# Rearranging the seams of a fused Fourier-mixing and mixture-of-experts kernel: start-up constants, the last two batches, the first expert tiles

## The chip, the cores and the metric

The kernel runs on one core of one Trainium2 chip. The metric is the device time of one execution in microseconds; lower is better. Beside the time stands a profile of one execution, with every instruction of the engines: PE (matrix multiply) with its weight loads PEld, DVE (VectorE), ACT (ScalarE), POOL (GpSimd), and the DMA queue of SP (SyncE).

## What is computed

Eight sequences of 2496 tokens with 256 channels go through a real Fourier transform along the sequence, a complex linear mix with a soft threshold, and the inverse transform. The 19968 result rows are tokens for a mixture of eight experts; each token goes to one expert, two matrix products with a ReLU between.

```python
X = np.fft.rfft(x, axis=1)
Yr = Xr @ w_r - Xi @ w_i + b_r
Yi = Xr @ w_i + Xi @ w_r + b_i
Yr = np.sign(Yr) * np.maximum(np.abs(Yr) - lam, 0.0)   # Yi likewise
y = np.fft.irfft(Yr + 1j * Yi, n=x.shape[1], axis=1)
...
logits = x @ w_gate + modality_bias[modality_id]
e_idx = np.argmax(logits, axis=1)
for e in range(E):
    h = np.maximum(x[mask] @ w1[e], 0.0)
    out[mask] = gate_w[mask, None] * (h @ w2[e])
```

## The kernel before

**Number format.** Products that need accuracy are made of three: a value is split into a high half (rounded copy, by ACT or DVE) and a low half (the value less its high half), and high·high, high·low and low·high are summed in PSUM.

**The Fourier part** runs over 8 batches (`b`). The transform is factored: `s1_chunk` (first forward stage, 11 chunks a batch, two batches ahead, its result stored to the DRAM scratch `scr` through the staging tile `ev`), `s2_pair` (second forward stage), the mix (`mix_bias`, `mix_shared`, `mix_own`, `shrink`), `is2_group` (first inverse stage, into the SBUF tile `z`), then 22 `pivot`s (transpose with the second inverse stage's split) and 22 `is1` (last stage and gate logits). A batch has a forward phase of five groups `g`, each with two pairs `m` and `m+1`, and then a pivot phase. The order of PE, ACT, DVE and POOL instructions is the order in which the code issues them; SP's order is set by the compiler's own schedule.

**PSUM.** Tags x (second forward stage), y (mix), z (first inverse stage and pivots) and r (last stage, routing) have two banks each. Odd pivots share y with the mix for `j < 16` and in the last two batches (line 369).

**Constants.** At `b == 0`, `g == 1` the generators `rt.consts()` and `at.consts_last()` take two tiles of the ring `ev` (three buffers in pool `w3`) as staging and load them by SP (lines 414, 196); at `g == 3` DVE copies them out and the buffers are free.

**Routing** of batch `b` (`Route.route`) is a generator of 14 small steps, mostly on DVE, run during batch `b+1`: `route()` takes one step unless the last one ended with "pe" (the next has a PE instruction); such a step waits until after `mix(m+1)` (lines 1141 to 1153). When it is done, 22 indirect DMAs a batch (`scatter`, POOL, line 548) write the rows of that batch, sorted by expert, into DRAM `xs`. For batch 5 the generator `tiles_early` (the table of expert tiles) follows the routing in the same chain; what is left of a chain goes on one step a pivot. `fence` makes SP wait for all scatters so far.

**Expert weights** are split by `SplitWeights.step` in 64 pieces: ACT makes the high half, POOL (in the forward groups) or DVE (in the pivot phase) the low half, two stores to DRAM `wsp` follow, and the next raw piece is loaded. Batch 7 has six of the steps.

**Seam between batches 6 and 7.** The banks y are held by odd pivots until the end of the pivot phase, so `mix_bias` for pairs 72 and 73 stands after the last pivot of batch 6; `fill` puts two matmuls of no use before it.

**Expert part** (`Experts.run`): 78 tiles of 256 tokens. SP loads the weights of tile 0, the tokens of tiles 0 to 3, and then, ordered behind the last scatter of batch 6 (line 927), the weights of tile 1. `prep` transposes a tile (DVE), makes its high half `xh` (ACT) and its low half `xl` (POOL, line 800); `ffn` has 48 matmuls from `xh` and `xl` (line 820) and 48 for the second product (line 850). The routing of batch 7 and its scatters run beside the first expert tiles. The pools of the expert part reuse the SBUF addresses of the Fourier part.

Of the kernel before, what the change touches and what calls it, by code (L numbers as in the profile page):

```python
# [128 lines left out]
class Attn:  # L129
# [5 lines left out]
    def pools(self, ctx):  # L135
        tc, nb = self.tc, self.nb
        pool = lambda name, bufs, **k: ctx.enter_context(tc.tile_pool(name=name, bufs=bufs, **k))

        self.w6 = pool("w6", 6)
        self.w3 = pool("w3", 3)  # L140
        self.wx = pool("wx", 3)
        self.ww = pool("ww", 2)
        self.wo = pool("wo", 2)
        self.cp = pool("consts", 1)
        self.w4 = pool("w4", 4)
        self.w2 = pool("w2", 2)
# [146 lines left out]
    def s2_pair(self, b, p, at):  # L293
        nc = self.nc
        ps = self.ps.tile([128, 2, 2, 2, N2], F32, tag="x", name=f"s2_{b}_{p}")
        for i in range(2):
            k1 = 2 * p + i
            for c in range(2):
                nc.tensor.matmul(ps[:, c, :, i, :], at[:, i, c * 128:(c + 1) * 128],
                                 self.m[:, k1 * 128:(k1 + 1) * 128].rearrange("p (r k) -> p r k", r=2),  # L300
                                 start=True, stop=True)
        ps = ps.rearrange("p c r i k -> p c r (i k)")
        us = self.w2.tile([128, 2, 128], F32, tag="Us", name=f"Us_{b}_{p}")
        xh = self.w3.tile([128, 2, 2, 128], F32R, tag="Xh", name=f"Xh_{b}_{p}")
        xl = self.w3.tile([128, 2, 2, 128], F32R, tag="Xl", name=f"Xl_{b}_{p}")
        nc.scalar.copy(us, ps[:, :, 0, :])
        nc.scalar.copy(xh, ps)
        nc.vector.tensor_add(us, us, ps[:, :, 1, :])
        nc.vector.tensor_sub(xl, ps, xh)
        return us, xh, xl  # L310

    def mix_bias(self, b, p):

        ps = self.ps.tile([128, 2, 256], F32, tag="y", name=f"mx_{b}_{p}")
        if b == self.nb - 1 and p in (2, 3):
            self.fill(ps)
        self.nc.scalar.copy(ps[:, 0, :], self.bias[:, 0, :])
        return ps

    def fill(self, ps):  # L320

        w = self.w.rearrange("p i c h d -> p (i c h d)")
        self.nc.tensor.matmul(ps.rearrange("p i d -> p (i d)"), w[:, :128], w[:, :512], start=True, stop=True)

# [23 lines left out]
    def is2_group(self, b, g, ss):  # L348

        nc = self.nc  # L350
        if g == 0:
            self.z = self.w1.tile([128, 2 * N2, K1, 2], F32, tag="z", name=f"z_{b}")
        ps = [self.ps.tile([128, 2, 2, 128], F32, tag="z", name=f"zs_{b}_{g}_{i}") for i in range(2)]
        for h, s in enumerate(ss):
# [11 lines left out]
    def pivot(self, b, j):  # L366
        nc = self.nc
        base = min(3 * j, N2 - 3)
        tag = "y" if j % 2 and (j < 16 or b >= self.nb - 2) else "z"
        ps = self.ps.tile([128, 512], F32, tag=tag, name=f"pv_{b}_{j}")  # L370
# [347 lines left out]
class Experts:  # L718
# [72 lines left out]
    def prep(self, i):  # L791
# [7 lines left out]
        nc.scalar.copy(xh, tr)  # L799
        nc.gpsimd.tensor_sub(xl, tr, xh)  # L800
        ix = self.x.tile([128, 2], I32, tag="ix", name=f"ix_{i}")
# [3 lines left out]
    def ffn(self, i, xh, xl, ix, between):  # L805
# [5 lines left out]
        for p in range(4):  # L811
# [4 lines left out]
            for q in range(2):  # L816
                f = 2 * p + q
                ops = [(lo, c, x) for lo, x in ((0, xh), (0, xl), (1, xh)) for c in range(2)]
# [182 lines left out]
def build(tc, I, out, nb):  # L1001
    nc = tc.nc
    with ExitStack() as outer:
        dp = outer.enter_context(tc.tile_pool(name="wsp", bufs=1, space=DRAM))
        wsp = dp.tile([E * 128, 8192], F32, name="wsp")
        with ExitStack() as ctx:
# [85 lines left out]

            state = None
            routing = iter(())

            def route(n=1):
                nonlocal state
                for _ in range(n):
                    if state != "pe":
                        state = next(routing, None)  # L1100

            for b in range(nb):
                done = b == nb - 1
                for g in range(5):
                    m = 10 * b + 2 * g + 2
                    if g or not b:
                        shared(m)
                        route()
                        shared(m + 1)
                    ins = load(m + 2) or ins  # L1110
                    ins = load(m + 3) or ins
                    if b == 0:
                        with tc.issue_after(ins.ins):
                            if g < 2:
                                at.table_load("m", g + 3)
                            if g < 4:
                                at.table_load("q", g + 1)
                            if g == 1:
                                late = [rt.consts(), at.consts_last()]
                            if g in (1, 3):  # L1120
                                for t in late:
# [19 lines left out]
                    due = state == "pe"  # L1141
# [6 lines left out]
                    if not due:  # L1148
# [3 lines left out]
                    if due:  # L1152
                        state = next(routing, None)
                    if g < 4:
                        bias(m + 2)
# [4 lines left out]
                    s2(m + 3)  # L1160
                    if g < 4:
# [7 lines left out]
                    route()  # L1169
# [11 lines left out]
                for j in range(J):  # L1181
# [9 lines left out]
                    if j == (20 if b + 2 < nb else J - 1):  # L1191
# [7 lines left out]
                for _ in routing:  # L1199
                    pass  # L1200
                shared(10 * b + 12)
                shared(10 * b + 13)
                for jj, r in pend:
# [47 lines left out]
```

## Time and profile before

| what | value |
|---|---|
| median of 3 runs | 1535.38 us (1535.17 to 1539.0) |
| profiled execution | 1536.55 us, of which the span from first to last instruction is 1534.8 us |
| PE busy | 1469.2 us (96%) |
| DVE, ACT, POOL busy | 722.9, 657.8, 510.7 us |
| pivot phases of batches 6 and 7 begin | 533.80 and 595.25 us |
| first expert matmul | 615.32 us |

Rows show a start, a duration, engine, line, operation and tiles; in square brackets the idle time before the instruction and what ended it. A `PEclk` of 1.00 or 0.50 is the granted TensorE clock: 2.4 or 1.2 GHz. A window row has the busy time of every engine in the stretch and, in brackets, how many instructions began there.

### The profile page before, as it was taken

The numbers are of one execution on the slowest core, as the hardware profiler recorded it, in microseconds if no ns is written. First come the engines' busy times: TensorE is split into PE (matmuls) and PEld (weight loads), VectorE is DVE, ScalarE is ACT, GpSimd is POOL, SyncE is SP. The second block draws the span as 40 slices with busy tenths as digits, with TensorE's granted clock in tenths as the row PEclk, the third lists the DMA queues.
The fourth block names the chain that finished last, engine by engine and source line by source line (L and its number), as shares of the span: only waits on it lengthen the run. The fifth ranks groups of instructions, "written<-read, shape, count | busy, mean of one in ns | idle before, by whom it ended". The sixth has DMA issues, their size and how long they took to land. (4 is left out here: it accounts for less than half of the span.)

```text
span 1534.8 us, 35125 instructions
## 1 busy us (share of the span) xinstructions
PE 1469.2 (96%) x12458; PEld 1420.7 (93%) x12458; DVE 722.9 (47%) x1546; ACT 657.8 (43%) x1375; POOL 510.7 (33%) x511
## 2 busy tenths in 40 slices
PE   4789999999999999799999999999999998999998
PEld 2689999999999988699999999999999998999998
DVE  3657767676776665343333333333333333333332
ACT  3347677777667556232323323232323222233232
POOL 0001344444445454335523223222322223223222
PEclk8899999999999999899999999999999999999999
DMA  6847687879786677423434325552225238626440
GB/s 193 250 140 239 223 272 229 285 227 295 229 266 193 199 223 224 160 54 79 129 69 115 90 51 162 156 156 43 57 43 161 49 63 302 207 41 199 122 145 35
DMA packets 289718, 244.58 MB, mean 159 GB/s; under 512 B 208448, under 2 KB 243980, under 8 KB 285289
## 3 DMA queue, kind: packets, MB, share of 16 engines
q1 hardware_dynamic: 270549, 200.73, 45.2%
q0 software_dynamic: 18992, 41.58, 8.1%
q8 instruction: 100, 1.64, 0.5%
q14 instruction: 77, 0.63, 0.1%
HBM read 432.83 MB, written 100.08 MB: 347 GB/s over the span
## 5 line engine op out<-in xcount | busy, mean ns | idle before, releaser
L850 PE MATMUL y<-w,hh 128*128 128x256 f32 x2496 | 433.3, 277 | 2.0 <-DMA w<-wsp 1.5
L820 PE MATMUL h<-xh,w 128*128 128x256 f32 x2496 | 403.7, 278 | 4.5 <-DMA w<-wsp 3.4
L850 PEld LDWEIGHTS y<-w,hh 128*128 128x128 f32 x2496 | 377.3, 188 | 2.8 <-ACT hh L822 2.3
L850 PE MATMUL y<-w,hl 128*128 128x256 f32 x1248 | 346.5, 278 | 0.1
L820 PEld LDWEIGHTS h<-xh,w 128*128 128x128 f32 x2496 | 340.2, 189 | 5.0 <-issue 3.6
L823 DVE SCALAR_TENSOR_TENSOR hl<-h,hh 128x512 fp32r<-128x512 f32 x312 | 209.5, 690 | 239.3 <-ACT hh L822 238.0
L863 POOL DMA_INDIRECT out<-o,ix x161 | 158.7, 985 | 429.8 <-ACT o L842 392.5
L820 PE MATMUL h<-xl,w 128*128 128x256 f32 x1248 | 245.7, 278 | 10.3 <-POOL xl L800 10.3
L822 ACT ACTIVATE hh<-h 128x512 fp32r<-128x512 f32 x312 | 178.7, 597 | 162.9 <-PE h L820 162.9
L850 PEld LDWEIGHTS y<-w,hl 128*128 128x128 f32 x1248 | 234.2, 188 | 0.8 <-DVE hl L823 0.3
L820 PEld LDWEIGHTS h<-xl,w 128*128 128x128 f32 x1248 | 189.8, 189 | 10.5 <-POOL xl L800 10.5
L840 DVE TENSOR_SCALAR o<-y,xt 128x256 f32<-128x256 f32 x78 | 37.8, 484 | 317.1 <-ACT o L842 313.0
L842 ACT ACTIVATE o<-y,xt 128x256 f32<-128x256 f32 x78 | 37.2, 477 | 345.7 <-PE y L850 345.7
L800 POOL TENSOR_TENSOR xl<-tr,xh 128x512 fp32r<-128x512 f32 x78 | 101.0, 1294 | 187.5 <-ACT xh L799 187.4
L548 POOL DMA_INDIRECT xs<-x1b,si x88 | 87.8, 998 | 83.8 <-ACT ph L378 30.5
L548 POOL DMA_INDIRECT xs<-x,si x88 | 87.8, 998 | 69.1 <-ACT u L344 25.4
L373 PE MATMUL pv<-pv,z 128*120 128x136 f32 x704 | 109.0, 279 | 1.8 <-DVE mid L455 1.8
L337 PE MATMUL mx<-wmix,Xh 128*128 128x256 f32 x640 | 104.8, 285 | 1.6 <-DVE mx L330 1.6
L373 PEld LDWEIGHTS pv<-pv,z 128*120 128x120 f32 x704 | 97.4, 182 | 8.2 <-ACT z L364 2.1
L379 DVE TENSOR_TENSOR pl<-pv,ph 120x264 fp32r<-120x264 f32 x176 | 76.0, 432 | 55.6 <-ACT ph L378 51.3
L995 POOL TENSOR_TENSOR wl<-wr,wh 128x512 fp32r<-128x512 f32 x46 | 59.1, 1286 | 124.7 <-ACT wh L994 118.9
L799 ACT CAST xh<-tr 128x512 fp32r<-128x512 f32 x78 | 48.5, 622 | 107.6 <-DVE ix L802 93.6
(191 smaller groups left out, 2119.9 us busy)
## 6 DMA issues: line engine op xcount, KB each, us to landing
w<-wsp SPq DMA_DIRECT2D x166, 2048.0 KB
a<-scr SPq DMA_DIRECT2D x80, 256.0 KB
xt<-xs SPq DMA_DIRECT2D x624, 32.0 KB
wr<-in_moe_w SPq DMA_DIRECT2D x64, 256.0 KB
wsp<-wh SPq DMA_DIRECT2D x64, 256.0 KB
wsp<-wl SPq DMA_DIRECT2D x64, 256.0 KB
scr<-ev SPq DMA_DIRECT2D x98, 160.0 KB
x<-in_x SPq DMA_DIRECT2D x96, 156.0 KB
```

The source lines that it names most:

```text
L337: self.nc.tensor.matmul(ps[:, i, :], t[:, c, 1 - i, :], self.w[:, i, c, lo, :], start=False, stop=n == len(ops) - 1, skip_group_check=True)
L373: nc.tensor.matmul(ps[:PK, c * 128:c * 128 + D // 2 + E], self.z[:, o:o + 3, :, :].rearrange("p n k r -> p (n k r)"), self.pv[:, c, :], st ...
L379: nc.vector.tensor_sub(pl, ps[:PK, :GC], ph)
L548: i = self.nc.gpsimd.indirect_dma_start(out=self.xs, out_offset=bass.IndirectOffsetOnAxis(ap=si[:, k:k + 1], axis=0), in_=rows, in_offset= ...
L799: nc.scalar.copy(xh, tr)
L800: nc.gpsimd.tensor_sub(xl, tr, xh)
L820: nc.tensor.matmul(ps[:, q, :], w1[:, lo, c, f * 128:(f + 1) * 128], x[:, c, :], start=n == 0, stop=n == 5)
L822: nc.scalar.activation(hh[:, 2 * p:2 * p + 2, :], ps, AF.Relu)
L823: nc.vector.scalar_tensor_tensor(hl[:, 2 * p:2 * p + 2, :], ps, 0.0, hh[:, 2 * p:2 * p + 2, :], ALU.max, ALU.subtract)
L850: nc.tensor.matmul(y[s], lhsT, w2[:, lo, f, :], start=n == 0, stop=n == 23)
L863: ins = self.nc.gpsimd.indirect_dma_start(out=self.out, out_offset=bass.IndirectOffsetOnAxis(ap=ix, axis=0), in_=o, in_offset=None, bounds ...
L995: eng.tensor_sub(lo, raw, hi)
```

## The change

- `xl` of expert tiles 0 and 1 is made by DVE, and tile 0 adds its low-half products last.
- The constants' generators start at `g == 2` and end at `g == 4`.
- In batches 6 and 7 (the last two) odd pivots use the banks x; batch 7's last group of `is2_group` uses x too. The pairs 72 and 73 get their bias in group 4 of batch 6, and `shared` for them stands before batch 6's pivots. `fill` is gone.
- Routing: a "pe" step is released by a count of `stage()` calls, six in a group, when it is over 2; in the last two batches three of the places in a group take two steps (`fast`).
- Weight splits: none in batch 7; batch 5 has seven instead of six in its groups; the pivot phases of batches 1 to 5 have three instead of two.
- Tiles `Xh` and `Xl` move to a pool of their own, `wX`, at other SBUF addresses.

```diff
+        self.wX = pool("wX", 3)
...
-        xh = self.w3.tile([128, 2, 2, 128], F32R, tag="Xh", name=f"Xh_{b}_{p}")
+        xh = self.wX.tile([128, 2, 2, 128], F32R, tag="Xh", name=f"Xh_{b}_{p}")
...
-        if b == self.nb - 1 and p in (2, 3):
-            self.fill(ps)
...
+        tag = "x" if b == self.nb - 1 and g == 4 else "z"
+        ps = [self.ps.tile([128, 2, 2, 128], F32, tag=tag, name=f"zs_{b}_{g}_{i}") for i in range(2)]
...
-        tag = "y" if j % 2 and (j < 16 or b >= self.nb - 2) else "z"
+        last = b >= self.nb - 2
+        tag = ("x" if last else "y") if j % 2 and (j < 16 or last) else "z"
...
-        nc.gpsimd.tensor_sub(xl, tr, xh)
+        (nc.gpsimd if i > 1 else nc.vector).tensor_sub(xl, tr, xh)
...
+                terms = ((0, xh), (0, xl), (1, xh)) if i else ((0, xh), (1, xh), (0, xl))
+                ops = [(lo, c, x) for lo, x in terms for c in range(2)]
...
+            def stage(n=1):
+                nonlocal state, age
+                age += n
+                if state == "pe" and age > 2:
+                    state, age = next(routing, None), 0
...
+                    fast = 1 + (b >= nb - 2)
                     if g or not b:
                         shared(m)
                         route()
+                        stage()
                         shared(m + 1)
+                        stage()
...
-                            if g == 1:
+                            if g == 2:
                                 late = [rt.consts(), at.consts_last()]
-                            if g in (1, 3):
+                            if g in (2, 4):
...
-                    route()
+                    route(fast)
                     s2(m + 2)
-                    steps = (b > 0) * min(2, max(0, (7 if b < 5 else 6) - 2 * g))
+                    stage()
+                    steps = min(2, max(0, (7 if b < 6 else 6) - 2 * g)) if 0 < b < nb - 1 else 0
...
                     mix(m + 1)
+                    stage()
...
-                    if g < 4:
+                    if g < 4 or b == nb - 2:
                         bias(m + 2)
...
-                    route()
+                    route(fast)
+                    stage()
                     at.is2_group(b, g, (ss.pop(m - 2), ss.pop(m - 1)))
...
-                    route()
+                    route(fast)
...
+                if b == nb - 2:
+                    shared(10 * b + 12)
+                    shared(10 * b + 13)
...
-                    if j in (8, 18) or b in (0, nb - 2) and j in (3, 13):
+                    if j in ((3, 8, 13, 18) if b in (0, nb - 2) else (4, 10, 15)):
                         sw.step(nc.vector)
```

## Rows read from the trace of the kernel before

**Rows 1.** Windows by stage: stretch, length, busy (count) per engine, PEclk, DMA, GB/s

```profile
480.00:520.00 40.00, 40.00 (x347) 37.83 (x346) 24.31 (x53) 25.58 (x60) 20.15 (x21) 1.00 0.78 255
...
600.00:640.00 40.00, 28.50 (x223) 27.70 (x222) 13.31 (x33) 16.14 (x45) 21.59 (x23) 0.83 0.66 198
1000.00:1200.00 200.00, 200.00 (x1725) 198.51 (x1724) 69.77 (x129) 61.27 (x113) 57.41 (x53) 1.00 0.34 87
```

**Rows 2.** Timeline of batch 0, 78 to 88 us: start, duration, instruction, [idle before]

```profile
78.46 0.33 SPq L197 DMA_DIRECT2D st_g<-in_c_g  x1
...
84.83 0.59 ACT L270 COPY ev<-s 120x512 f32<-120x512 f32 x1 [7.33 <-DMA scr<-ev]
...
87.84 3.78 PE L329 MATMUL mx<-wmix_r,Us 128*128 128x256 f32 x8 [4.84 <-ACT mx L317]
```

**Rows 3.** Windows of chosen stretches, columns as in the first group

```profile
117.75:144.51 26.76, 26.76 (x192) 25.00 (x191) 19.36 (x43) 21.21 (x55) 1.28 (x3) 1.00 0.70 227
187.17:213.84 26.67, 26.67 (x192) 24.95 (x191) 18.11 (x41) 20.52 (x53) 13.19 (x15) 1.00 0.74 235
533.80:553.64 19.84, 19.51 (x150) 18.23 (x150) 16.61 (x62) 12.27 (x34) 12.82 (x16) 1.00 0.64 206
595.25:612.79 17.54, 17.54 (x148) 17.54 (x148) 9.07 (x23) 13.34 (x40) 13.78 (x16) 1.00 0.81 228
...
86.94:93.76 6.82, 5.92 (x19) 5.20 (x20) 4.27 (x8) 3.91 (x10) 0.00 (x0) 0.50 0.60 190
...
626.12:629.65 3.53, 3.53 (x16) 3.53 (x17) 0.30 (x1) 0.60 (x1) 0.00 (x0) 0.50 0.59 190
626.67:633.30 6.63, 6.63 (x47) 6.63 (x46) 2.54 (x6) 1.69 (x3) 0.00 (x0) 0.78 0.87 339
```

**Rows 4.** Timeline of PE at the seam of batches 6 and 7, and after batch 7

```profile
533.80 0.69 PE L373 MATMUL pv<-pv,z 128*120 128x136 f32 x4 [0.91 <-DVE mid L455]
...
553.64 0.39 PE L323 MATMUL mx<-wmix 128*128 128x512 f32 x1
...
554.95 1.89 PE L329 MATMUL mx<-wmix_r,Us 128*128 128x256 f32 x8
...
613.70 0.38 PE L385 MATMUL i<-ph,c_g 120*117 120x264 f32 x1 [0.21 <-ACT x L388]
```

**Rows 5.** Waits of PE, 553 to 596 us: in total, times, longest

```profile
PE mx L337 <- DVE mx L330: 1.3, 2, 1.1
PE mx L329 <- ACT mx L317: 0.9, 1, 0.9
...
PE zs L360 <- ACT z L364: 0.7, 1, 0.7
```

**Rows 6.** Timeline of DVE, POOL and ACT around routing steps and weight splits

```profile
564.94 2.68 DVE L489 TENSOR_TENSOR L<-L,mx 117x176 f32<-117x176 f32 x1
564.92 2.49 POOL L995 TENSOR_TENSOR wl<-wr,wh 128x512 fp32r<-128x512 f32 x2
571.60 0.62 ACT L994 CAST wh<-wr 128x512 fp32r<-128x512 f32 x1 [3.82 <-issue]
542.59 1.00 POOL L548 DMA_INDIRECT xs<-x,si  x1 [0.30 <-ACT wh L994]
542.69 0.68 DVE L995 TENSOR_TENSOR wl<-wr,wh 128x512 fp32r<-128x512 f32 x1
```

**Rows 7.** Timeline from batch 7's third group to the first expert tile

```profile
580.17 0.69 ACT L344 ACTIVATE u<-mx,nlam 128x512 f32<-128x512 f32 x1 [0.54 <-PE mx L337]
594.90 1.09 POOL L548 DMA_INDIRECT xs<-x1b,si  x1 [8.66 <-issue]
623.78 0.99 POOL L548 DMA_INDIRECT xs<-x1b,si  x1 [0.30 <-issue]
626.12 0.80 PE L820 MATMUL h<-xl,w 128*128 128x256 f32 x2 [10.30 <-POOL xl L800]
626.67 12.84 SPq L763 DMA_DIRECT2D w<-wsp  x4
```

More of the change, by code (lines that the diff above doesn't have):

```diff
@@ L303, in s2_pair @@
         us = self.w2.tile([128, 2, 128], F32, tag="Us", name=f"Us_{b}_{p}")
-        xh = self.w3.tile([128, 2, 2, 128], F32R, tag="Xh", name=f"Xh_{b}_{p}")
-        xl = self.w3.tile([128, 2, 2, 128], F32R, tag="Xl", name=f"Xl_{b}_{p}")
+        xh = self.wX.tile([128, 2, 2, 128], F32R, tag="Xh", name=f"Xh_{b}_{p}")
+        xl = self.wX.tile([128, 2, 2, 128], F32R, tag="Xl", name=f"Xl_{b}_{p}")
         nc.scalar.copy(us, ps[:, :, 0, :])
@@ L314, in mix_bias @@
         ps = self.ps.tile([128, 2, 256], F32, tag="y", name=f"mx_{b}_{p}")
-        if b == self.nb - 1 and p in (2, 3):
-            self.fill(ps)
         self.nc.scalar.copy(ps[:, 0, :], self.bias[:, 0, :])
         return ps
-    def fill(self, ps):
-        w = self.w.rearrange("p i c h d -> p (i c h d)")
-        self.nc.tensor.matmul(ps.rearrange("p i d -> p (i d)"), w[:, :128], w[:, :512], start=True, stop=True)
     def mix_shared(self, ps, us):
@@ L352, in is2_group @@
             self.z = self.w1.tile([128, 2 * N2, K1, 2], F32, tag="z", name=f"z_{b}")
-        ps = [self.ps.tile([128, 2, 2, 128], F32, tag="z", name=f"zs_{b}_{g}_{i}") for i in range(2)]
+        tag = "x" if b == self.nb - 1 and g == 4 else "z"
+        ps = [self.ps.tile([128, 2, 2, 128], F32, tag=tag, name=f"zs_{b}_{g}_{i}") for i in range(2)]
         for h, s in enumerate(ss):
@@ L817, in ffn @@
                 f = 2 * p + q
-                ops = [(lo, c, x) for lo, x in ((0, xh), (0, xl), (1, xh)) for c in range(2)]
+                terms = ((0, xh), (0, xl), (1, xh)) if i else ((0, xh), (1, xh), (0, xl))
+                ops = [(lo, c, x) for lo, x in terms for c in range(2)]
                 for n, (lo, c, x) in enumerate(ops):
@@ L1091, in build @@
             s2(3)
-            state = None
+            state, age = None, 0
             routing = iter(())
             def route(n=1):
-                nonlocal state
+                nonlocal state, age
                 for _ in range(n):
                     if state != "pe":
-                        state = next(routing, None)
+                        state, age = next(routing, None), 0
+            def stage(n=1):
+                nonlocal state, age
+                age += n
+                if state == "pe" and age > 2:
+                    state, age = next(routing, None), 0
             for b in range(nb):
@@ L1140, in build @@
                     route()
-                    due = state == "pe"
                     if b == 0:
@@ L1146, in build @@
                     mix(m)
+                    stage()
                     rt.scatter(1 if b < nb - 2 or g < 3 else 2, at.mark)
-                    if not due:
-                        route()
+                    route()
                     mix(m + 1)
+                    stage()
                     rt.scatter(1 if b < nb - 2 or g < 2 else 2, at.mark)
-                    if due:
-                        state = next(routing, None)
-                    if g < 4:
+                    if g < 4 or b == nb - 2:
                         bias(m + 2)
@@ L1160, in build @@
                     s2(m + 3)
-                    if g < 4:
+                    if g < 4 or b == nb - 2:
                         bias(m + 3)
@@ L1164, in build @@
                         sw.step(nc.gpsimd)
-                    route()
+                    route(fast)
+                    stage()
                     at.is2_group(b, g, (ss.pop(m - 2), ss.pop(m - 1)))
@@ L1190, in build @@
                         at.is1(b, jj, *r, nc.scalar.copy if done or jj % 2 else nc.vector.tensor_copy)
-                    if j == (20 if b + 2 < nb else J - 1):
+                    if j == 20 and b + 2 < nb:
                         bias(10 * b + 12)
                         bias(10 * b + 13)
-                    if j in (8, 18) or b in (0, nb - 2) and j in (3, 13):
+                    if j in ((3, 8, 13, 18) if b in (0, nb - 2) else (4, 10, 15)):
                         sw.step(nc.vector)
@@ L1200, in build @@
                     pass
-                shared(10 * b + 12)
-                shared(10 * b + 13)
+                if b < nb - 2:
+                    shared(10 * b + 12)
+                    shared(10 * b + 13)
                 for jj, r in pend:
```

1 line of the change is left out of this document (removed).

## The prediction, made before the changed kernel was built

> **What bounds the kernel now.** I read the busy shares of the page first, then PE's waits, then windows by stage, then the timeline of each gap. PE is the bound: in a whole batch's stretch and in the expert part it is busy without a gap at the full clock, with DVE, ACT and POOL at 30 to 64% there [rows 1]. An edit inside those stretches therefore moves nothing while PE stays fed; what can be won lies in stretches where PE stands still or has the lower clock. There are four that the change touches: the start-up around 83 to 94 us [rows 2, 3], the seam of batches 6 and 7 [rows 4], batch 7's groups [rows 5], and the passage to the experts, 600 to 640 us, where PE has 28.50 of 40 us [rows 1, 7]. The start-up before 60 us, where loads of x end the waits, is not edited.
>
> **Part 1, constants a group later.** The chain is plain in the timeline. At 78.46 SP gets past the load into `st_g`, which had to wait for a staging buffer of the ring `ev`; the stores of scratch rows behind it on SP are late by that. ACT stands 7.33 us at its copy into `ev`, since the ring's two other buffers went to constants. Behind that copy on ACT are the threshold and the bias copies, and PE stands 4.84 us for a bias [rows 2]. Then the clock falls: from 86.94 to 93.76 PE has 0.50, with 5.92 us of work [rows 3]. With the generators a group later, chunk 10's `ev` takes the buffer whose store ended long ago, and the constants take buffers of stores that are then over. Gone: 4.84, and of 5.92 us at half speed at most 2.96; I take 2.5, since PE also waited there for 0.9 us. Sum 7.3. Bounds: 0 (another wait ends at the same place) to 7.8. The six constant loads pass behind the group's own loads on SP, and the DVE copies move from group 3 to group 4; DVE has room there as in [rows 1], so I cost them at nothing; if that cover were missing, some 2 us.
>
> **Part 2, seam of batches 6 and 7.** (a) Before batch 6's pivots PE stands 0.91 us for the copies of `z` [rows 4]; the eight `shared` matmuls, 1.5 us and more, now stand there and cover it: 0.9. (b) From 553.64 to 554.95 PE has the two fills and a wait: 1.31 gone [rows 4]. But `shared` also covered the latency of the last pivots, and what is late next is the last `is1`, as at the end of batch 7, where the step that starts at 613.70 is some 0.4 us late [rows 4]. Net 0.9. (c) Batch 6's 22 pivots take 19.84 us, batch 7's 17.54; in 6 DVE is busy 16.61 with 62 instructions, some 20 of them steps of the tile table [rows 3]. With two steps at three places a group, 31 of the chain's 36 steps are over before the pivots. The DVE copies of `is1` and the four splits stay, so not all of 2.30 goes: I take 1.0 (0 to 2.3). Sum 2.8 (0.9 to 4.1). Pivots in x instead of y have as many banks as before.
>
> **Part 3, batch 7's groups.** PE's waits are 1.3, 0.9 and 0.7 us [rows 5]. The first: a routing subtraction on DVE took 2.68 us while POOL made two low halves of weights back to back [rows 6], and DVE's additions behind it were late for PE. The second: ACT stood 3.82 us before a weight piece [rows 6], with the threshold and bias behind it. Without splits in batch 7 both go. The third is the bank z at two `is2` groups in a row, which the x banks resolve. Sum 2.9 (1 to 3.5); batch 6's groups, with six splits, show no gap [rows 1], so a stage without splits should not have one.
>
> **Part 4, first expert tiles.** PE stands 10.30 us for `xl`, because POOL works off 22 scatters first, from 594.90 to 623.78, back to back 0.99 + 0.30 = 1.29 us each; then 3.53 us run at half clock [rows 3, 7]. DVE is idle then and makes `xl` in the 0.68 us of its own equal subtraction [rows 6]. `xl` follows `xh`, and with the low products last PE has four matmuls, 0.5 us, before it needs it: a rest of 0.3 us. Gain 10.0 + 1.7 = 11.7 (9.5 to 12).
> What is late next is the weights of tile 1, which wait on SP for the last scatter. Before, SP issued at 626.67, 1.9 us after the last scatter's end, and the first layer's 2 MB were in by about 633.30 at 339 GB/s, 6.6 us [rows 3, 7]. After: by the same count of steps batch 6's routing ends in batch 7's third group, so the first scatters follow the threshold that ran at 580.17 [rows 7], some 14 us ahead of the pivots. Eleven scatters go in the groups, held by POOL's 1.29 and by the threshold of each mix, and end some 5 us into the pivots; bias products take 1.6 us, eleven more take 14.2. The last ends about 20.5 us after the pivots begin, the pivot phase itself 19.1. So the weights are issued some 3.3 us after the last `is1`, in 6.6 us later, at 9.9. Tile 0 begins 1.0 us after the last `is1` and has 96 matmuls at 200 / 1725 = 0.116 us, so tile 1 begins at 12.4. Margin 2.5 us: no wait.
>
> **Part 5, weight splits moved.** Five pivot phases get one step more, 0.63 us of ACT and 0.68 of DVE. Batch 0 has four steps in its phase and takes 26.76, batch 1 has two and takes 26.67 [rows 3]: 0.05 us a step, 0.2 in all, taken as 0. The new routing places in batches 1 to 5 are likewise covered by PE.
>
> **Sum.** 7.3 + 2.8 + 2.9 + 11.7 = 24.7 us. The profiled execution took 1536.55, so 1511.9; the median of the runs lies 1.2 lower, so **1510.7**.
>
> One rule of the skill speaks against a place of part 2. Shown first: the subtraction with both inputs in SBUF took 2.68 us beside POOL's two subtractions, while DVE's split beside a scatter took its usual 0.68 [rows 6]. The Trainium skill, "SBUF — State Buffer", section "Who interferes with whom", says that a VectorE instruction with two SBUF inputs contends with a GpSimd instruction that reads SBUF, and one blocks the other for its whole length. The trace agrees for POOL's subtractions; for scatters it shows no such block. In batch 6 the same subtraction now stands right behind a POOL split. By the rule it would be blocked there, and at the 1.1 us of PE that this cost in batch 7 the sum would be 23.6.
>
> **Rivals.**
> (A) The start-up gap is only renamed: the load of scratch rows or the constants' copies in group 4 end a wait of the same length. For it: DMA is at 0.60 there [rows 3]; against: nothing but `ev` was late in the chain. 1510.7 + 7.3 = 1518.0.
> (B) The change doesn't bring the scatters forward, because each is tied to the newest ACT result and POOL is in order. Then with 13.0 us won before it, SP issues at 626.67 - 13.0 = 613.7, weights are in at 620.3, and tile 1 would want them at 615.3 - 13.0 + 0.3 + 11.1 = 613.7: 6.6 us of waiting and some 1.7 of clock, 1519.0.
> (C) The two-input block hits batch 6's routing, or `xl` beside a scatter: 1.1 us, 1511.8.
> (D) Slower: the pivot splits at j = 4, 10, 15 find their raw piece not loaded, and ACT stands before each as it did for 3.82 us [rows 6], with the `ph` copies of the pivots behind it. 15 steps at 3.8 are 57 us, 1568. It makes the kernel slower from 24.7 / 15 = 1.6 us a step on. Against it: batch 0 has them closer and pays 0.05 a step [rows 3].
>
> **How the numbers follow.** Forecast 0.62, A 0.13, B 0.13, C 0.07, D 0.03, the change without effect 0.02. All upper bounds together give 27.4, so 1508; the runs shown differ by 3.8 us, which I add in part: low end 1505. The high end takes in A and B with some spread, 1521, and leaves out both at once. A difference over 0.3%, 4.6 us, is what a measurement of this kernel can tell from none. Faster: the forecast, A, B and C, 0.95, less 0.01 for sums that shrink: 0.94; same 0.03; slower 0.03.
>
> **What would show it.** Right: no ACT wait at the copy into `ev` near 78 us and full clock to 100 us; `shared` ahead of batch 6's pivots; no wait over 0.5 us in batch 7's groups; first scatter of batch 6 some 14 us ahead of batch 7's pivots; tile 0's first low-half product under 1 us after its first product, clock 1.00; tile 1 without a wait for weights. Wrong: a DMA wait of PE at tile 1 (B), a new wait of 3 us or more between 80 and 120 us (A), pivot phases of batches 1 to 5 over 27 us (D).

## The result and the profile after

The changed kernel takes **1515.4 us** (median of 4 runs, 1513.87 to 1515.97) beside 1535.28 us of the kernel before on the same chip: a ratio of 0.9866, with a 95% interval of 0.9846 to 0.9885. That is 19.9 us less where the prediction had 24.7; the time lies within its range. The profiled execution took 1515.97 us, with a span of 1514.2.

The stages below are read off the timeline of TensorE in the two profiled executions. A stage of pivots begins with the first product of the first pivot and ends with the last product of the last `is1`; a forward stretch is what lies between two of them. The forecast is that of the prediction's parts.

| stage | before, us | after, us | difference | forecast |
|---|---|---|---|---|
| start to batch 0's pivots | 117.75 | 111.34 | -6.4 | -7.3 |
| forward stretches of batches 1 to 5, sum | 213.85 | 217.86 | **+4.0** | 0 |
| pivots of batches 0 to 5, sum | 160.18 | 160.17 | 0.0 | 0 |
| batch 6, forward and pivots | 65.80 | 65.17 | **-0.6** | -2.8 |
| batch 7's forward stretch | 37.68 | 33.40 | -4.3 | -2.9 |
| batch 7's pivots | 19.07 | 19.06 | 0.0 | 0 |
| last `is1` to the first expert tile | 0.99 | 1.03 | 0.0 | 0 |
| first expert tile to the second | 24.11 | 12.30 | -11.8 | -11.7 |
| the other expert tiles | 895.35 | 893.89 | -1.5 | 0 |

So the two largest gains came out near their forecasts, a loss of 4 us stands where none was seen, and the seam gave a quarter of what it was to give.

Windows of the changed kernel (stretch, length, busy time and count of each engine, granted clock, DMA share, GB/s): around the group where the old gap stood, batch 3's forward stretch, batch 6's forward stretch and its pivots, batch 7's forward stretch, the first expert tile.

```profile
74.00:90.00 16.00, 16.00 (x148) 15.08 (x147) 10.77 (x21) 9.11 (x19) 0.49 (x2) 1.00 0.66 216
...
278.61:322.14 43.53, 42.61 (x404) 40.12 (x404) 32.37 (x67) 28.64 (x61) 19.77 (x20) 1.00 0.84 273
...
489.37:533.32 43.95, 43.27 (x407) 40.58 (x407) 32.10 (x83) 25.25 (x55) 23.02 (x23) 1.00 0.68 219
533.32:553.15 19.83, 19.50 (x149) 17.97 (x147) 15.60 (x44) 12.31 (x35) 12.90 (x16) 1.00 0.61 194
554.54:587.94 33.40, 32.49 (x334) 30.84 (x333) 20.91 (x48) 16.32 (x35) 8.51 (x11) 1.00 0.65 201
608.02:620.32 12.30, 12.30 (x102) 11.97 (x102) 6.51 (x16) 3.52 (x7) 0.80 (x1) 1.00 0.69 268
```

In the first row TensorE has no idle time and the full clock where it stood 4.84 us before and then ran at 0.50 [rows 2, 3]; the same holds from 80 to 100 us. In the second it has 42.61 us of work in 43.53. Before, batch 3 had gaps of 0.29 us and the other four of batches 1 to 5 none; these are batches 2 and 3 of the kernel before (TensorE's busy time alone, clock, DMA share, GB/s):

```profile
213.84:256.62 42.78, 42.78 (x404) 1.00 0.84 269
283.30:326.38 43.08, 42.79 (x403) 1.00 0.85 276
```

The fourth row answers to batch 6's 22 pivots in [rows 3]: DVE has 44 instructions instead of 62, and the stage takes the same 19.83 us (19.84).

Waits of TensorE in the changed kernel from 117 to 615 us (what waits, for what: us in total, times, longest):

```profile
PE mx L331 <- DVE mx L324: 4.1, 7, 0.9
PE h L817 <- ACT xh L795: 1.0, 1, 1.0
PE pv L369 <- DVE mid L451: 0.9, 1, 0.9
PE rt L505 <- DVE oh L500: 0.6, 1, 0.6
```

The first is the new one: products of the mix wait for DVE's addition of the bias, in batches 1 to 5. Of its 4.1 us, 3.3 stand 27.7 us into the stretch, once in each batch (0.38 to 0.92 us); the other 0.8 stand 18.7 us into batches 2 and 4. Here is the wait in batch 1, as DVE, GpSimd and TensorE have it (start, us, instruction, [idle before, and what ended it]):

```profile
162.60 1.28 POOL L992 TENSOR_TENSOR wl<-wr,wh 128x512 fp32r<-128x512 f32 x1 [3.80 <-ACT wh L991]
162.67 0.33 DVE L528 TENSOR_REDUCE sl<-rk 117x22 f32<-117x176 f32 x1
163.03 0.89 DVE L530 TENSOR_TENSOR si<-sl,inv 117x22 int32<-117x22 f32 x1
163.84 0.68 DVE L359 COPY z<-zs 128x512 f32<-128x512 f32 x1
164.44 0.67 DVE L248 TENSOR_TENSOR x1l<-x,x1h 117x512 fp32r<-117x512 f32 x1
165.04 0.32 DVE L534 TENSOR_REDUCE sm<-ex 117x22 f32<-117x176 f32 x1
165.29 0.42 DVE L324 TENSOR_TENSOR mx<-mx,bias 128x256 f32<-128x256 f32 x1
...
165.76 0.72 PE L331 MATMUL mx<-wmix,Xh 128*128 128x256 f32 x4 [0.81 <-DVE mx L324]
```

Ahead of the addition at 165.29 DVE has three steps of the routing, a copy of `z` and a split. One of the steps, 117 x 22 elements, took 0.89 us: it began while GpSimd subtracted a weight's low half and ended with it. TensorE stood 0.81 us. In the kernel before, the same addition of batch 1 had the copy and the split ahead of it and no step of the routing, and the step of 117 x 22 elements came 10 us later and took 0.18 us:

```profile
168.47 0.68 DVE L364 COPY z<-zs 128x512 f32<-128x512 f32 x1
169.56 0.69 DVE L247 TENSOR_TENSOR x1l<-x,x1h 117x512 fp32r<-117x512 f32 x1 [0.41 <-ACT x1h L246]
170.17 0.76 DVE L330 TENSOR_TENSOR mx<-mx,bias 128x256 f32<-128x256 f32 x2
```

The passage to the experts in the changed kernel:

```profile
607.83 0.99 POOL L544 DMA_INDIRECT xs<-x1b,si  x1 [0.30 <-issue]
608.00 0.69 DVE L796 TENSOR_TENSOR xl<-tr,xh 128x512 fp32r<-128x512 f32 x1 [0.68 <-ACT xh L795]
608.02 0.74 PE L817 MATMUL h<-xh,w 128*128 128x256 f32 x4 [1.03 <-ACT xh L795]
608.75 0.51 PE L817 MATMUL h<-xl,w 128*128 128x256 f32 x2
...
611.74 8.66 SPq L759 DMA_DIRECT2D w<-wsp  x4
...
620.32 0.48 PE L817 MATMUL h<-xh,w 128*128 128x256 f32 x2
```

The scatters of batch 6 begin at 575.88, 12.05 us before batch 7's pivots (the prediction had some 14), where they began at 594.90 [rows 7]. The last now ends at 608.82, 20.9 us after the pivots begin (the prediction counted 20.5), where it ended at 624.77 before [rows 7]. `xl` is there when the first low product wants it, and the second tile begins without a wait.

### The profile page after: what moved, and what is told of

It is laid out like the page before. It is cut to its first block, busy times and chain, and to the rows that moved or that the text cites. A ratio compares the mean times of both kernels' runs of the same rounds, so it can differ in the third digit from the quotient of the medians.

```text
span 1514.2 us, 35138 instructions
## 1 busy us (share of the span) xinstructions
PE 1461.7 (97%) x12456; PEld 1413.0 (93%) x12456; DVE 732.7 (48%) x1553; ACT 654.7 (43%) x1375; POOL 501.8 (33%) x504
## 5 line engine op out<-in xcount | busy, mean ns | idle before, releaser
L300 PE MATMUL s<-c_m,a 128*128 128x128 f32 x640 | 85.6, 277 | 8.2 <-DMA a<-scr 8.2
```

## The experiments

Twelve kernels, in three groups of four, each group on a chip of its own beside the kernel before (medians of before: 1533.65, 1536.94 and 1554.35 us). Ratios are to the kernel before on the same chip; sums of forward stretches are those of batches 1 to 5, as in the table.

**First group: which part of the change did what.** The routing of batches 1 to 5 at its old places (no new places for `stage`, no second step at a place, the old `due` rule):

```diff
-                if state == "pe" and age > 2:
+                if new and state == "pe" and age > 2:
...
-                    fast = 1 + (b >= nb - 2)
+                    new = b >= nb - 2
+                    fast = 1 + new
...
+                    due = not new and state == "pe"
...
-                    route()
+                    if not due:
+                        route()
...
+                    if due:
+                        state = next(routing, None)
```

> The changed kernel, with the old placing of routing steps in batches 0 to 5 (a step marked pe waits for the end of the second mix, one less place for a step) and the new placing in batches 6 and 7 alone. Theory O (order on DVE): the forward phases of batches 1 to 5 grew from 42.7 to 43.5 us because routing steps now stand on DVE between the splits and the additions that the mix waits for; here they fall back to 42.6 to 42.9, PE's waits for the mix additions go from 4.1 to under 0.5 us, and the time to 1511.4 (1510 to 1513). Rival S (the moved weight splits: batch 5's seventh, the third in each pivot phase, and what they shift on POOL and SP): the phases stay at 43.4 or more and the time at 1515.

It took 1514.7 us, ratio 0.9891 (0.9858 to 0.9925). Batches 1 and 5 fell to 42.47 and 42.69 us, as the theory of the routing places has it, but batches 2 to 4 took 43.91, 44.98 and 46.37, more than with the change: two batches went the way of that theory and three the way of its rival. The longest, in batch 4, by the waits of ACT and TensorE from 353 to 363 us:

```profile
ACT wh L991 <- DMA wr<-in_moe_w: 3.4, 1, 3.4
...
PE mx L323 <- ACT mx L316: 1.9, 1, 1.9
```

ACT stands before the cast of a raw weight (`wh`, from `wr`) that hasn't landed, with the threshold and the bias copies behind it, and TensorE waits for the bias. That is the mechanism of the prediction's rival D, not in the pivots but after them. So a second theory is needed, and the second group asks it.

The low halves of the weights written as zeros by GpSimd (they are left out of the result), so that it reads nothing from SBUF there:

```diff
-        eng.tensor_sub(lo, raw, hi)
+        if eng is nc.gpsimd:
+            nc.gpsimd.memset(lo.bitcast(F32), 0.0)
+        else:
+            eng.tensor_sub(lo, raw, hi)
```

> The changed kernel; in the forward groups POOL writes zeros in place of the weights' low halves (so this part of the expert products is left out), an instruction that reads nothing from SBUF. Rival C (contention): DVE's steps with two SBUF inputs are blocked by POOL's subtraction (0.89 instead of 0.18 us, 1.40 instead of 0.33), and that makes the waits of PE in batches 1 to 6; then the forward phases of batches 1 to 5 fall from 43.5 to about 42.8 and the time to 1511.5. Theory O: the order alone does it, blocks are at most half; phases stay at 43.1 to 43.5, time 1513.5 to 1515.5. Either way the blocked steps are back at 0.18 and 0.33 us.

1512.11 us, ratio 0.9861 (0.9839 to 0.9884). Its batches 3 and 6, in windows, and the same step as above beside GpSimd's write, in batch 2:

```profile
278.99:321.83 42.84, 42.47 (x403) 39.93 (x403) 30.42 (x67) 28.75 (x61) 13.66 (x19) 1.00 0.85 276
489.05:531.74 42.69, 42.69 (x407) 40.35 (x407) 29.52 (x83) 25.14 (x55) 17.78 (x22) 1.00 0.70 223
...
234.25 0.53 POOL L993 MEMSET wl<- 128x512 f32 x1
234.38 0.18 DVE L530 TENSOR_TENSOR si<-sl,inv 117x22 int32<-117x22 f32 x1
```

The step takes 0.18 us again, in all eight batches (0.18 to 0.20; with the change 0.88 or 0.89 in batches 1 to 5), though in batches 2 to 5 GpSimd's write lies over all of it. The wait 27.7 us into the stretch is gone from all five batches, with the steps in the same order, so at that place the cost is the block and not the order alone. Batch 6's stretch is 1.26 us shorter than 43.95, and without a gap. But raw weights were late again (13.0 us of ACT's waits in seven places), and the stretches of batches 1 to 5 took 47.05, 44.45, 42.84, 43.44 and 43.71 us: the 42.8 expected came in batch 3 alone. The 0.37 us that TensorE still stands there come 18.6 us into the stretch, after the stretch's third cast of a weight had waited 1.34 us for its raw piece. The two gaps of 0.42 us at that place with the change follow third casts that were 1.5 us late, and a kernel with the old routing (the first of the third group) has one of 0.37 us behind a cast 0.35 us late. So these gaps aren't the routing's.

The first tiles' `xl` by GpSimd again:

```diff
-        (nc.gpsimd if i > 1 else nc.vector).tensor_sub(xl, tr, xh)
+        nc.gpsimd.tensor_sub(xl, tr, xh)
```

> The changed kernel with the low halves of tiles 0 and 1 back on POOL; the order of tile 0's products stays. The forecast booked 10 us of the wait to the change of engine. Theory E (the earlier scatters did most): POOL is free at 608.8, xl is done at 610.2, PE waits 1.5 to 2 us at tile 0 and the clock stays at 1.00: time 1517 (1516 to 1518.5). Rival V (the engine did it): POOL still has the scatters ahead of it, PE waits 8 to 10 us and half clock follows: 1525.

1516.75 us, ratio 0.9901 (0.9878 to 0.9923). First tile to second: 15.03 us instead of 12.30.

```profile
609.16 0.79 PE L817 MATMUL h<-xl,w 128*128 128x256 f32 x2 [1.44 <-POOL xl L796]
...
607.90:613.00 5.10, 3.84 (x20) 3.85 (x21) 0.94 (x2) 0.60 (x1) 1.20 (x1) 0.67 0.36 85
```

The wait is 1.44 us, where before the change it was 10.30, and the granted clock of the stretch is 0.67 (1.00 was expected). The scatters, which begin some 19 us earlier than before, took away most of that wait; DVE's part, with its clock, is 2.7 us.

The old routing in all batches (the first edit, with another value):

```diff
-                    new = b >= nb - 2
+                    new = False
```

> The changed kernel with the old placing of routing steps in all batches, one step a place, so that batch 6's scatters start only at batch 7's last group; xl stays on DVE. Theory W (the weights of tile 1 take over as the limit): the last scatter is issued some 10 us after the last product of batch 7, PE waits 6 to 8 us for the first layer's weights at tile 1, and with the 4 us that batches 1 to 5 give back the time is 1518 to 1520. Rival N (the wait for the weights is covered): no wait at tile 1, time 1511.

1527.41 us, ratio 0.9952 (0.9931 to 0.9974), where 1518 to 1520 were expected. Batch 6's stretch fell to 42.71 us, batch 7's rose to 35.86, and the first tile to the second took 20.52:

```profile
629.02 0.77 PE L817 MATMUL h<-xh,w 128*128 128x256 f32 x2 [8.09 <-DMA w<-wsp]
```

With late scatters DVE's `xl` doesn't help: the weights of the second tile, on SP behind the last scatter, are late by 8.1 us. That is rival B, at a higher price than the prediction gave it: the wait alone is 8.1 for 6.6, and the clock behind it, for which it had 1.7, is 0.50 from 629 to 633 us, which the 20.52 doesn't count. The full gain of 11.8 us needs both: earlier scatters and `xl` off GpSimd's queue.

**Second group: routing places, split places, start-up.** The changed kernel again, with no edit:

> The changed kernel itself, unedited, beside the other runs of this chip. Two theories of the 4.0 us that the forward stretches of batches 1 to 5 lost: R, the new routing places (two steps of routing and a split stand in DVE ahead of the bias additions; TensorE waits for these), and S, the new places of the weight splits (three in each stage of pivots instead of two, the last of them at pivot 15; SP's queue is then late with the next raw weights, and ACT's cast at the head of the next forward stretch waits for them). R: forward stretches 43.5 to 43.7 us in batches 1 to 5 as in the first profile of this kernel, ACT waits for raw weights under 1 us in all. S: ACT waits for raw weights 4 us or more in all, as in the two edited kernels with the same places of splits, and the stretches vary from 43.5 to 45. Median 1514 to 1516 us either way.

1517.64 us, ratio 0.9884 (0.985 to 0.9918). The stretches of batches 1 to 5 took 43.52 to 44.37 us, and ACT waited 7.1 us in four places for raw weights, both as S has it. In the first profile of the same kernel it waited 2.5 us in two, in batches 4 and 5:

```profile
ACT wh L991 <- DMA wr<-in_moe_w: 2.5, 2, 1.5
```

The splits as before (two in the pivots of batches 1 to 5, six in batch 7):

```diff
-                    steps = min(2, max(0, (7 if b < 6 else 6) - 2 * g)) if 0 < b < nb - 1 else 0
+                    steps = (b > 0) * min(2, max(0, (7 if b < 5 else 6) - 2 * g))
...
-                    if j in ((3, 8, 13, 18) if b in (0, nb - 2) else (4, 10, 15)):
+                    if j in (8, 18) or b in (0, nb - 2) and j in (3, 13):
```

> The changed kernel with the weight splits where they stood before (two in the pivots of batches 1 to 5, six in batch 7), all else as changed. R: forward stretches of batches 1 to 5 stay at 43.4 to 43.7 us. S: 42.6 to 43.0 us, and no wait of ACT for raw weights. Both: batch 7's forward stretch gets longer than 33.40 us by 0 (the prediction's term: the six splits are covered) to 2.7 us (its six casts on ACT at 0.64 are on the path with nothing beside them, 3.8, less what was idle). Time against the changed kernel: R +0 to +2.7, S -4 to -1.

1523.27 us, ratio 0.9923 (0.9897 to 0.995): 5.6 us over the changed kernel, more than either theory had. The stretches took 43.53 to 43.61, steady, as R has it. Batch 7's stretch grew by 1.2 us, and the rest of the loss was somewhere neither theory looked. Batch 2's stretch in a window, then SP's queue and the second tile:

```profile
207.56:251.09 43.53, 42.73 (x403) 40.06 (x403) 32.46 (x67) 28.64 (x61) 19.62 (x20) 1.00 0.83 264
...
581.60 0.33 SPq L994 DMA_DIRECT2D wsp<-wl  x1
...
585.80 13.78 SPq L777 DMA_DIRECT2D xt<-xs  x8
...
618.20 2.48 SPq L759 DMA_DIRECT2D w<-wsp  x4
...
625.74 0.77 PE L817 MATMUL h<-xh,w 128*128 128x256 f32 x2 [4.93 <-DMA w<-wsp]
```

The stores of the last splits hold SP until 581.60; the loads of the first four tiles' rows come behind them, and the second tile's weights only at 618.20, 4.9 us too late, though the last scatter, which they wait for too, had ended at 609.28. In the changed kernel those loads are issued from 572.11 to 594.42 and the weights at 611.74. The second tile began 17.44 us after the first, beside 12.30 and 13.82 in the two profiles of the changed kernel. Taking the splits out of batch 7 thus carries 3.6 to 5.1 us of the passage to the experts, and beyond it the granted clock is 0.50 from 625.74 to 631 us.

Both undone together, that edit and the first one of the first group:

> Both undone: routing of batches 1 to 5 and all splits as before; the start-up, batch 6, batch 7's groups and the transition as changed. R and S: the forward stretches of batches 1 to 5 return to the 42.66 to 43.08 us of the kernel before, no wait of ACT for raw weights over 1 us; time 3 to 4 us under the changed kernel, less what the six splits cost in batch 7 (0 to 2.7). If the stretches still vary between 42.5 and 46 us, neither of the two places is the cause, and what varies is the DMA traffic of the run.

```profile
208.04:250.45 42.41, 42.41 (x403) 40.02 (x403) 30.61 (x67) 28.83 (x61) 19.58 (x20) 1.00 0.87 273
277.14:319.78 42.64, 42.64 (x404) 40.20 (x403) 30.59 (x67) 28.82 (x61) 19.63 (x20) 1.00 0.87 280
```

All five stretches at 42.41 to 42.64 us, TensorE without a gap; ACT waited 0.9 us for raw weights. The sum of the five in all runs that bear on it:

| | splits at the old places | splits at the changed places |
|---|---|---|
| routing at the old places | 212.5 (the kernel before: 213.9) | 218.3, 220.4, and 213.4 on the third chip |
| routing at the changed places | 217.7 | 217.9, 219.0, 219.1, 219.4 |

Down the left column the routing places cost 5.2 us, 1.0 to 1.1 a batch, with one profile each and raw weights late in neither by more than 2.8 us of ACT's time. In the right column the routing's cost doesn't show beside that of the splits. Across the table the split places cost 0 to 8 us, and not the same in two runs of the same code. The time was 1517.75 us, ratio 0.9881 (0.9856 to 0.9906), no better than the changed kernel beside it, where 3 to 4 us less were expected. In the profiled executions, 1521.31 us beside 1516.38, the five stretches won 6.8 us, but batches 6 and 7 took 1.8 more, the second tile came 3.8 later, the other tiles took 3.5 more, and the pivots of batch 0 began 2.8 later, which the edit doesn't touch.

The constants at groups 1 and 3 again:

```diff
-                            if g == 2:
+                            if g == 1:
                                 late = [rt.consts(), at.consts_last()]
-                            if g in (2, 4):
+                            if g in (1, 3):
```

> The changed kernel with the constants of the routing at groups 1 and 3 of batch 0 again. Prediction's theory (SP's queue stands at the load of the constants, and ACT and TensorE behind it): the first pivots begin 7 to 8 us later than in the changed kernel on this chip, the gap of some 4.8 us with no matmul is back between 78 and 90 us and the half clock after it; time 6 to 8 us over the changed kernel. Rival A (the gap comes from something else and only moved): no more than 2 us over it.

1524.52 us, ratio 0.9924 (0.99 to 0.9947), 6.9 us over the changed kernel. ACT's copy and TensorE's bias product as in [rows 2], and the clock behind them:

```profile
85.20 0.58 ACT L271 COPY ev<-s 120x512 f32<-120x512 f32 x1 [9.10 <-DMA scr<-ev]
88.21 3.78 PE L323 MATMUL mx<-wmix_r,Us 128*128 128x256 f32 x8 [6.70 <-ACT mx L316]
...
85.00:93.00 8.00, 4.79 (x18) 4.08 (x19) 4.92 (x9) 4.79 (x10) 0.00 (x0) 0.57 0.60 185
```

From the first product of batch 0's second transform to the first pivot it took 74.83 us, with the change 67.65 on this chip: 7.2 us, near the prediction's 7.3.

**Third group: is there a better version?** The chip of this group is slower for every kernel (before: 1554.35 us), and on it even stages that the edits don't touch are longer: batch 7's pivots 21.66 us and more instead of 19.06. Only ratios and the forward stretches of batches 1 to 5 are compared with the other groups. All four have the routing of batches 1 to 5 at the old places, and batch 6's copies on ACT:

```diff
-                        at.is1(b, jj, *r, nc.scalar.copy if done or jj % 2 else nc.vector.tensor_copy)
+                        at.is1(b, jj, *r, nc.scalar.copy if b >= nb - 2 or jj % 2 else nc.vector.tensor_copy)
```

> The changed kernel with the routing of batches 1 to 5 at its old places and the copies of batch 6's last products all on ACT, as in batch 7; the splits stay at the changed places. Batch 6's pivots: the copies on DVE are what keeps them at 21.2 us (22 pivots of 0.85 or more), so with the copies on ACT 19.1 to 19.4 as in batch 7; if the copies are not the cause, 21.2. Forward stretches: R (routing places) alone would give 42.4 to 42.7 us in batches 1 to 5; with S (split places) still there some of them are longer, up to 46, with ACT waits for raw weights of 4 us or more in all. Time 1510 to 1517 us.

1540.1 us, ratio 0.9905 (0.9869 to 0.994). Stretches 42.48 to 42.97 us with the changed split places, and only 0.2 us of waits for raw weights: this time the split places cost nothing. Batch 6's pivots took 23.16 us, 1.5 over batch 7's on this chip, where it was 2.2 over with copies on both engines (21.22 and 19.06). From batch 0's pivots on TensorE waited 3.4 us in three places for ACT's copies of `x1b`, 0.3 with the change. What the copies are worth stays open, since the change itself wasn't run on this chip.

Eight splits in the forward stretches, two in the pivots:

```diff
+                    steps = min(2, max(0, (8 if b < 6 else 6) - 2 * g)) if 0 < b < nb - 1 else 0
...
+                    if j in ((3, 8, 13, 18) if b in (0, nb - 2) else (8, 18)):
```

> As the last, but with two splits in the pivots of batches 1 to 5 (at 8 and 18, as before the change) and eight instead of seven in their forward stretches, so that none is left for batch 7. S: forward stretches of batches 1 to 5 at 42.4 to 42.9 us, ACT waits for raw weights under 2 us in all; the eighth split beside DVE costs at most 0.4 a batch. Batch 7's forward stretch 33.3 us and the first tile to the second 12.3 to 13.8 us, as in the changed kernel, since no split stands on SP's queue ahead of the tile loads. Time 1508 to 1512 us, 5 to 8 under the changed kernel on the same chip (1517.6, its own runs 1513 to 1521).

1538.35 us, ratio 0.9888 (0.986 to 0.9917). Four stretches at 42.50 to 42.66 us, one at 44.06; first tile to second 12.30. The 1508 to 1512 us expected can't be read against this chip; by its ratio it is no faster than the changed kernel.

Six splits in batch 0's pivots, seven in batch 6's, two in the others:

```diff
+                    if j in {0: (3, 6, 9, 12, 15, 18), nb - 2: (2, 5, 8, 11, 14, 17, 20)}.get(b, (8, 18)):
```

> As the last, but the splits that the forward stretches took go into the pivots of batch 0 (six) and of batch 6 (seven). S: forward stretches of batches 1 to 5 at 42.4 to 42.7 us but for batch 1's, which follows six splits in the pivots and starts with SP late: up to 44. Batch 6's pivots with ACT's copies and seven casts of 0.63: 19.3 to 21. Time 1508 to 1513 us.

1545.43 us, ratio 0.993 (0.9905 to 0.9955). Stretches of batches 1 to 5 42.53 to 42.65, but batch 0's pivots took 32.41 us instead of 26.75, and batch 6's 26.70 where 19.3 to 21 were expected. Batch 0's pivots in a window, then the waits of ACT and TensorE from 110 to 143 us:

```profile
110.17:142.58 32.41, 28.62 (x192) 26.30 (x191) 20.37 (x45) 21.88 (x57) 1.28 (x3) 0.95 0.75 246
...
ACT wh L991 <- DMA wr<-in_moe_w: 4.3, 2, 3.5
...
PE pv L369 <- DVE pl L375: 3.5, 2, 2.9
```

This is rival D as the prediction drew it: with a split every three pivots the raw piece isn't there, ACT stands up to 3.5 us, and the pivots behind it wait. With the change's distance of five or six it didn't come.

No split in batch 6's forward stretch, seven in the pivots of batches 0 and 6, eight in the forward stretches of batches 1 to 5:

```diff
+                    steps = min(2, max(0, 8 - 2 * g)) if 0 < b < nb - 2 else 0
...
+                    if j in ((2, 5, 8, 11, 14, 17, 20) if b in (0, nb - 2) else (8, 18)):
```

> As the eight-split kernel, but batch 6's forward stretch has no split (seven in the pivots of batch 0 and of batch 6 instead). If the steps of routing in batch 6 are long because GpSimd subtracts beside them (a step of 0.33 us took 1.1 to 1.4 there), batch 6's forward stretch falls from 43.9 to 42.5 to 42.9 us; if the number of steps alone makes it long, it stays at 43.6 or more. Pivots of batch 6 19.3 to 21. Time 1507 to 1512 us.

1543.07 us, ratio 0.9915 (0.9887 to 0.9944). Batch 6's stretch took 46.06 us, missing the 42.5 to 42.9 expected on this chip, but 2.2 to 2.4 less than in the three beside it (48.28 to 48.41): without GpSimd's subtraction it is shorter, as with the zeros above, but here ACT's casts are gone too, and which of the two it is isn't told apart. Its stage of pivots took 27.23 us, where 19.3 to 21 were expected, and batch 0's 31.93. No version tried beats the changed kernel.

## Why the prediction was right, and where it missed

**Part 1, right.** 7.2 us by undoing it, 7.3 forecast; the windows show 8.0 from batch 0's second transform to the pivots in the two profiled executions, of which 1.6 are lost because that transform began later, at 43.5 instead of 41.9 us: up to there TensorE waited 8.2 us for scratch rows instead of 7.2, and 0.9 us more for pieces of x, in a part that nothing edited. Rival A is out: the gap isn't renamed, the row of 74 to 90 us has none.

**Part 2, right in place, too large.** The wait before the pivots is gone (0.9), and so are the fills, with the last `is1` 0.42 us late as the prediction said: from the last full pivot to the end, `shared` left out, 2.04 became 1.39 us, 0.65 for 0.9. The term that failed is (c): 18 fewer steps on DVE took nothing off the 22 pivots, 19.84 to 19.83 us. DVE's steps weren't what makes batch 6's pivots longer than batch 7's; what does stays open. And batch 6's forward stretch, 42.03 us before, should have been 43.11 with `shared` in it (1.99) and the wait out of it (0.91), and took 0.84 more: steps of 0.33 us took 1.12 and 1.40 beside GpSimd's subtractions, and TensorE stood 0.65 us for `oh`, the last of that chain. The second of them and the chain on DVE, beside a subtraction on GpSimd from 496.58 to 497.85:

```profile
496.64 1.40 DVE L491 SCALAR_TENSOR_TENSOR fr<-L,rev 117x176 f32<-117x176 f32 x1
497.97 0.68 DVE L359 COPY z<-zs 128x512 f32<-128x512 f32 x1
498.57 0.32 DVE L494 TENSOR_REDUCE rm<-fr 117x22 f32<-117x176 f32 x1
498.93 0.34 DVE L500 SCALAR_TENSOR_TENSOR oh<-fr,rm 117x176 bf16<-117x176 f32 x1
```

That is rival C, which the prediction had at 1.1 us for this very place; with zeros in place of the subtraction the stretch had no gap.

**Part 3, right, too small.** TensorE's idle time in batch 7's stretch fell from 4.03 us to 0.91, 3.1 for 2.9 forecast; the rest is the wait before the pivots that stood there before. The other 1.2 us are pace: the same 334 products were busy 33.65 us before and 32.49 after, and why isn't shown. Nor is it shown which part of the change took the old waits away. With the six splits back the stretch was 1.2 us longer, and with the old routing 2.5, but none of the old waits returned in either: 0.56 us of the first was a wait for a routing step, 1.9 of the second one for scratch rows. No run undoes the x banks or the pool `wX` alone.

**Part 4, right in sum, with the wrong shares.** 11.8 for 11.7, and the signs that were named were there, with the first scatter 12 us ahead of the pivots for some 14: full clock, first low product 0.73 us after the first product, the weights issued 4.75 us after the last `is1` (forecast 3.3), no wait at the second tile. But the sum was credited to DVE's `xl`, 10.0, with the order of the scatters as a mere margin. The runs show that DVE's part is 2.7 us with the scatters early, that it brings at most 3.6 in the passage (24.11 to 20.52) with the scatters late, and that the margin of the weights is made by two other parts: the routing, 8.1 us of wait without it, and the splits out of batch 7, 4.9 without that. The prediction gave the move of the splits no part in this. The sum came out right because the change holds all three, not because the credit was.

**Part 5, wrong: this is the step that failed.** "The new routing places in batches 1 to 5 are likewise covered by PE" cost 4.0 us in the first profile and 5.2 by the left column of the table. The reason given was the mean: TensorE busy without a gap, DVE at 24.31 of 40 us [rows 1]. But a place decides what stands ahead of a due instruction, and a mean busy share doesn't show order. Some 27 us into a stretch three routing steps came to stand ahead of a bias addition, where none stood before, and one of them right beside a subtraction on GpSimd, so that it lasted until that ended. With zeros for the subtraction the same order left no wait there. The Trainium skill, "SBUF — State Buffer", section "Who interferes with whom", which the prediction weighed for batch 6 alone, says that a VectorE instruction with two SBUF inputs and one of GpSimd that reads SBUF exclude each other; the trace agrees, with 0.89 us beside the subtraction and 0.18 without it. The prediction priced this once, at 1.1 us; it came back in each of five batches (0.38 to 0.92 us of TensorE's time).
The split half of part 5 was right for the pivots (26.68 us each, as before) and is not settled for the forward stretches behind them: late raw weights cost between 0 and some 8 us there, and runs of one code differ. In the first profile of the changed kernel 0.8 of the 4.1 us of waits stand behind late casts, so the routing's part is 3.3. That the three splits a stage have to do with it is supported by the 0.9 and 2.8 us of ACT's waits for raw weights with two of them, beside 4.1 to 13.0 in six profiles with three, but not by the 2.5 us in the first profile of the changed kernel and the 0.2 us on the third chip, with three as well. What decides it in a given run stays open.

Of the 24.7 us forecast: 0.9 less in part 1 with the later loads, 2.2 less in part 2, 1.4 more in part 3, 0.1 more in part 4, 4.0 lost in part 5, 1.5 more in the later expert tiles: 20.6, the difference of the two spans. Nothing edits those tiles and the cause of the 1.5 us is open; they took 892.2 to 899.1 us in the other kernels of the first two chips. That the total came so near is in part luck: the 1.4 and 1.5 us that nobody forecast offset two fifths of what parts 1, 2 and 5 fell short by.

## What to carry to other kernels

Busy shares say how much room an engine has, not where: before an instruction is moved onto an engine with room, read in the timeline which due instruction it will stand ahead of, and what runs on the other engine beside it. Multiply by the number of batches before calling it nothing. And when a wait is taken away at the end of a chain, ask of every other load on the same queue when it was issued: here the routing's new places and the splits' new places in batch 7 each kept the second tile's weights on time, and undoing the one or the other made them 8.1 or 4.9 us late.

## What the runs showed of the hardware

On the third chip engines were idle without a visible releaser. The waits from 100 to 640 us (DVE, then TensorE) of the kernel with eight forward splits:

```profile
DVE s L339 <- issue: 11.7, 16, 0.8
DVE Us L309 <- issue: 6.9, 17, 0.6
...
PE zs L355 <- issue: 4.7, 9, 1.1
```

On the first chip of the experiments, in the kernel with the old routing, DVE had 0.7 us of such idle time in that stretch, in three places, and TensorE none. The one instruction compared, the threshold on ACT, took 0.689 us on the second chip and on the third, so for it the time between instructions grew and not their length; why is open.
